# Attention, soft mixture of experts and a gated output layer on one core: a matmul wake-up at the start, two reordered weight loads and a rewritten end of attention

## The chip, the core and the metric

The kernel runs on one core of a Trainium2 chip. TensorE (PE) multiplies, VectorE (DVE), ScalarE (ACT) and GpSimd (POOL) work on tiles in the on-chip memory, and SyncE (SP) does nothing but issue DMA transfers, in program order. Sixteen DMA engines share out every transfer. The metric is the device time of one execution in microseconds. Before the change it is 331.34 us, the median of three runs (331.23, 331.34 and 331.82).

## What is computed

Three stages follow each other on 3072 tokens of 512 columns, all in float32 (the weights `w_in` and `w_out` of the last stage arrive in 64-bit floats and are converted on the chip).

```python
# 1 chunked attention: 4 batches x 8 heads x 768 positions x 64; 24 chunks of 32 queries
for c in range(nc):                       # each chunk sees 8 memory keys and up to 56 keys around it
    scores = scale * np.matmul(q_c, k_full.transpose(0, 1, 3, 2))
    a = softmax(scores)                   # max subtracted, exp, divided by the sum + 1e-9
    out[:, :, c_start:c_end] = np.matmul(a, v_full)
x = attn_out as [3072, 512]
# 2 soft mixture of 8 experts with 4 slots each
logits = x @ phi                          # [3072, 32]
d = softmax over the 3072 tokens;  slot_input = d.T @ x
slot_out[e] = np.maximum(slot_input[e] @ w1[e], 0.0) @ w2[e]
x = softmax over the 32 slots @ slot_out
# 3 output layer
h = x @ w_in;  solu = h * softmax(h);  ln = layer norm of solu * g_ln
return ln @ w_out
```

## The kernel before

Attention runs over 32 groups (`GROUPS`), each of 3 tiles of 128 query rows, for one pair of heads in half a batch. One block of keys and queries (`load_qk`, line 187, 400 KB) is loaded for each group into one of four buffers, and one block of values for two groups (`load_v`, line 201, two transfers of 390 KB) into one of two buffers. The loop over `g` issues, in this order: the scores of group g+1 (`emit_qk`, PE, L281), its softmax on DVE and ACT, the load of the keys four groups ahead, weight loads as the list `LOADS[g]` says (in units of 512 KB), the product with the values of group g-1 (`emit_pv`, PE, L337), for even g the load of the values two to three groups ahead, then transposes (`emit_t` L319, `emit_xt` L348) and copies. `emit_spread` copies the keys into a padded layout three groups ahead (ACT L326, DVE L328, POOL L330). Every four groups form a half batch `hb`, for which the logits (`emit_lg`, L360), their running maximum, and a rescaled sum of slot inputs (`emit_dacc`, L407 and L421) are made.

After the loop the last three groups are finished by hand, the four partial sums are merged (`merge_max`, `merge_sum`, `merge_end`) and `emit_slots` gives the slot inputs. Then the 16 half experts run (`emit_w1` L524, `emit_ht` L531, `emit_w2` L542), with the conversion of `w_out` and the softmax over slots beside them. Then the last stage runs over 24 tiles on PE (L747).

The order of everything is the order of the code (`tc.manual_schedule`). Weights go into slots of 512 KB or 1 MB (`load_e`, lines 255 and 258); a slot is used again when `release` says that its weights were consumed. When attention has used a buffer for the last time, its room is given to weights too: `ex0` is the room of the keys, `ex1` that of the values, `ex2` and `ex3` two of the blocks `x`. A transfer is issued when its target is free and when the transfer eight places ahead of it has landed; SP waits there, and everything behind it on SP's queue waits with it.

```python
LOADS = [0, 0, 0, 2, 0] + [0, 2] * 6 + [0, 1] + [0, 2] * 5 + [99, 99, 0, 0]
...
            if g + 4 < GROUPS:
                load_qk(g + 4)
            load_e(LOADS[g])
            if 1 <= g:
                emit_pv(g - 1)
            if g % 2 == 0 and 0 < g and g // 2 + 1 < GROUPS // 2:
                load_v(g // 2 + 1)
```

Of the kernel before, what the change touches and what calls it, by code (L numbers as in the profile page):

```python
# [43 lines left out]
LOADS = [0, 0, 0, 2, 0] + [0, 2] * 6 + [0, 1] + [0, 2] * 5 + [99, 99, 0, 0]  # L44
# [3 lines left out]
C_ID, C_I4, C_REP, C_NM, C_PHI, C_G = 0, 128, 160, 288, 289, 417  # L48
NCONST = 425
# [16 lines left out]
TORD = [1, 0]  # L66
TKEEP = [2, 1]
# [11 lines left out]
def tile_kernel(ctx: ExitStack, tc: tile.TileContext, kr, vr, w1, w2, w_in, w_out, cst, out):  # L79
# [323 lines left out]
    def emit_dacc(hb, b=7, steps=(0, 1)):  # L403
        n = 32 * GT
        alpha = alphas[hb % 2]
        for t in range(GT if 0 in steps else 0):
# [3 lines left out]
        if 1 not in steps:  # L410
            return
        if hb == 0:
            dve.tensor_copy(out=acc[0:n], in_=bank(b)[0:n])
        else:
            (pool if hb < HB - 1 else dve).tensor_scalar(
                out=ssum[0:n], in0=ssum[0:n], scalar1=alpha[0:n], scalar2=snews[hb % 2][0:n],
                op0=ALU.mult, op1=ALU.add,
            )
            if hb == HB - 1:
                merge_sum()  # L420
            dve.scalar_tensor_tensor(  # L421
                out=acc[0:n], in0=acc[0:n], scalar=alpha[0:n], in1=bank(b)[0:n], op0=ALU.mult, op1=ALU.add
            )
# [398 lines left out]
    with tc.manual_schedule():  # L822
        for i in range(4):
            (pool if i < 3 else dve).memset(at("vz", 2 * VS * i, 2 * VS), 0.0)
            if i < 2:
                dve.memset(kz[i][0:64, KS:2 * KS], 0.0)
                dve.memset(kz[i][64:128, 0:KS], 0.0)
        load_qk(0)
        act.dma_start(out=at("cst", 0, NCONST), in_=cst)
# [5 lines left out]
        load_e(2)  # L835
# [28 lines left out]
        for g in range(GROUPS):  # L864
            if g + 1 < GROUPS:
                emit_qk(g + 1)
# [19 lines left out]
            if g + 1 < GROUPS:  # L886
                emit_exp(g + 1)
# [10 lines left out]
        area("x2", [("ex2", 1024)])  # L898
        more("ex2", 1)
        emit_softmax(GROUPS + 1)  # L900
        emit_dmax(HB - 2)
        emit_xt(GROUPS - 3)
        emit_pv(GROUPS - 1)
        emit_dexp(HB - 2)
        emit_softmax(GROUPS + 2)
        emit_xt(GROUPS - 2, 0)
        if TORD[0]:
            emit_xt(GROUPS - 1, 1)
        emit_turned_pe([dtb, ptb])
        emit_turned_act([Db, l_of(HB - 2)])  # L910
        if not TORD[0]:
            emit_xt(GROUPS - 1, 1)
# [107 lines left out]
def layout(inputs):  # L1020
# [31 lines left out]
    c = np.zeros((P, NCONST), f)  # L1052
# [2 lines left out]
    c[p, C_I4 + p % 32] = 1.0
    for r in range(4):
        c[p, C_REP + 32 * r + p % 32] = 1.0
# [26 lines left out]
```

## Time and profile before

| what | value |
|---|---|
| median of three runs | 331.34 us |
| the profiled execution, its own time | 331.76 us |
| its span in the trace | 330.0 us (1.76 us lie around it) |
| PE busy | 298.8 us, 91% |
| DVE / ACT / POOL busy | 72% / 67% / 51% |
| chain that ended last, by engine | PE 61%, DMA 18%, DVE 9% |
| bytes moved by DMA | 95.85 MB |

All times below are microseconds from the start of the span. Attention lasts until about 118, the experts until 171, the last stage from there to the end. The busy share of PE is an average over stages with different limits, and its matmuls are pipelined, so 91% busy is not 91% of its peak. The stage by stage view is in the stretches and in the chain of waits.

### The profile page before, as it was taken

To read this page: it belongs to the slowest core of one execution; us is meant where nothing else is said; L and a number is where in the kernel's file an instruction comes from. 1 tells how busy PE (TensorE), PEld (TensorE's weight loads), DVE (VectorE), ACT (ScalarE), POOL (GpSimd) and SP (SyncE) were. 2 spreads that over 40 slices of the span, in tenths; PEclk is the share of its full clock that TensorE was granted. 3 is DMA by queue.
4 is the path that set the end of the run, shared out by engine and by line. 5 is a ranking of instruction groups with operands and counts; after the bars stand their busy time and mean duration, and the time that the engine had idled before them with its cause. 6 is when DMAs were issued, how large, how long until landed. Compare 5 with 4: busy or idle time off the path is not lost.

```text
span 330.0 us, 8289 instructions
## 1 busy us (share of the span) xinstructions
PE 298.8 (91%) x3069; PEld 217.0 (66%) x3069; DVE 236.9 (72%) x431; ACT 222.5 (67%) x441; POOL 169.1 (51%) x395
## 2 busy tenths in 40 slices
PE   2787989898898799879899899999999999999996
PEld 2576767677676433333335688888888888888885
DVE  6675888886877339998027986888878788787540
ACT  3566756865775446785326789998888888888721
POOL 5255577666675022233100457777767676666600
PEclk9999999999999999999999999999999999999999
DMA  7999999999999999999930005675656756576521
GB/s 291 422 368 411 412 415 420 413 420 414 416 403 412 392 422 428 422 423 423 422 148 0 1 34 195 240 264 199 234 218 219 251 203 219 219 237 238 194 95 65
DMA packets 32696, 95.85 MB, mean 290 GB/s; under 512 B 3856, under 2 KB 14480, under 8 KB 28944
## 3 DMA queue, kind: packets, MB, share of 16 engines
q1 hardware_dynamic: 32512, 95.11, 74.0%
q8 instruction: 24, 0.39, 0.5%
q10 hardware_dynamic: 144, 0.22, 0.2%
q14 instruction: 16, 0.13, 0.1%
HBM read 78.53 MB, written 16.78 MB: 289 GB/s over the span
## 4 chain that ended last, share of the span: by engine, by line
PE 61%; DMA 18%; DVE 9%; POOL 3%; issue 3%; ACT 2%; SPq 1%; POOLq 0%; ACTq 0%; DVEq 0%
PE bank L747 37%; DMA kq_area<-in_kr_dram 9%; DMA ex_area<-in_w_dram 5%; PE bank L281 5%; PE bank L337 4%; DMA e_area<-in_w_dram 4%; PE h L659 4%; POOL kq_area L330 3%; PE bank L319 2%; SPq L201 1%; PE bank L348 1%; PE bank L360 1%; PE bank L407 1%; PE bank L524 1%; PE bank L757 1%
## 5 line engine op out<-in xcount | busy, mean ns | idle before, releaser
L747 PE MATMUL bank<-wh_area,yh_area 128*128 128x512 f32 x552 | 129.8, 390 | 0.0
L747 PEld LDWEIGHTS bank<-wh_area,yh_area 128*128 128x128 f32 x552 | 103.4, 188 | 21.7
L330 POOL TENSOR_SCALAR kq_area<-kq_area 64x416 f32<-64x416 f32 x88 | 38.3, 440 | 36.2 <-DMA kq_area<-in_kr_dram 21.1
L281 PE MATMUL bank<-kq_area 128*32 128x128 f32 x768 | 29.4, 288 | 14.3 <-POOL kq_area L330 7.3
L322 ACT COPY s_area<-bank 128x384 f32<-128x384 f32 x32 | 15.3, 477 | 32.7 <-PE bank L319 31.4
L730 DVE STREAM_TRANSPOSE yq_area<-yq_area 128x1024 f32<-128x1024 f32 x20 | 24.9, 1245 | 17.2 <-DMA yq_area<-z 17.2
L674 DVE SCALAR_TENSOR_TENSOR eb_area<-h,eb_area 128x1024 f32<-128x1024 f32 x24 | 29.1, 1217 | 9.5 <-ACT eb_area L668 9.2
L281 PEld LDWEIGHTS bank<-kq_area 128*32 128x32 f32 x768 | 20.6, 114 | 20.6 <-POOL kq_area L330 10.7
L299 DVE TENSOR_REDUCE cst_area<-bank 128x6 f32<-128x384 f32 x32 | 17.8, 555 | 19.5 <-PE bank L281 19.0
L337 PE MATMUL bank<-vz_area,s_area 128*32 128x130 f32 x768 | 28.7, 274 | 3.3 <-issue 1.2
L712 POOL TENSOR_SCALAR cst_area<-cst_area 128x1 f32<-128x1 f32 x72 | 26.6, 370 | 7.6
L665 DVE TENSOR_REDUCE cst_area<-h 128x1 f32<-128x1024 f32 x24 | 29.0, 1217 | 0.9 <-PE h L659 0.9
L701 POOL TENSOR_SCALAR cst_area<-cst_area 128x1 f32<-128x1 f32 x24 | 16.9, 705 | 22.4 <-ACT eb_area L668 20.5
L668 ACT ACTIVATE eb_area<-h,cst_area 128x1024 f32<-128x1024 f32 x24 | 26.7, 1112 | 1.9 <-DVE cst_area L665 1.9
L697 ACT ACTIVATE eb_area<-eb_area,cst_area 128x1024 f32<-128x1024 f32 x24 | 27.3, 1139 | 0.1
L694 ACT ACTIVATE eb_area<-eb_area,cst_area 128x1024 f32<-128x1024 f32 x20 | 23.1, 1154 | 4.8 <-DVE eb_area L674 4.3
L741 DVE TENSOR_TENSOR yh_area<-yq_area,yh_area 128x1024 fp32r<-128x1024 f32 x20 | 24.5, 1226 | 2.3 <-ACT yh_area L737 2.3
L337 PEld LDWEIGHTS bank<-vz_area,s_area 128*32 128x32 f32 x768 | 21.6, 108 | 5.8 <-issue 2.2
L737 ACT CAST yh_area<-yq_area 128x1024 fp32r<-128x1024 f32 x20 | 21.0, 1049 | 5.4 <-DVE yq_area L730 5.3
L713 POOL TENSOR_SCALAR cst_area<-cst_area 128x1 f32<-128x1 f32 x72 | 19.9, 276 | 7.1
L765 ACT ACTIVATE eb_area<-bank,cst_area 128x512 f32<-128x512 f32 x23 | 15.8, 687 | 9.7 <-POOL cst_area L703 7.0
L314 ACT ACTIVATE s_area<-s_area 128x384 f32<-128x384 f32 x32 | 16.9, 530 | 2.4 <-DVE s_area L305 2.3
(153 smaller groups left out, 526.9 us busy)
## 6 DMA issues: line engine op xcount, KB each, us to landing
e_area<-in_w_dram SPq DMA_DIRECT2D x15, 1024.0 KB, 10.4
kq_area<-in_kr_dram SPq DMA_DIRECT2D x32, 400.0 KB, 7.3
vz_area<-in_vr_dram SPq DMA_DIRECT2D x32, 390.0 KB, 6.6
ex_area<-in_w_dram SPq DMA_DIRECT2D x10, 1024.0 KB, 14.8
z<-eb_area SPq DMA_DIRECT2D x20, 512.0 KB, 2.8
yq_area<-z SPq DMA_DIRECT2D x80, 128.0 KB, 2.9
out_dram<-eb_area SPq DMA_DIRECT2D x23, 256.0 KB, 2.0
e_area<-in_w_in_dram SPq DMA_DIRECT2D x4, 1024.0 KB, 9.0
```

The costliest lines, as they stand in the source:

```text
L281: pe.matmul(out=bk[32 * j:32 * j + 32, t * 128:(t + 1) * 128], lhsT=kq[i][:, KT + c * CH:KT + (c + 1) * CH], rhs=kwin(g % 2, c), start=Tru ...
L330: pool.tensor_scalar(out=o, in0=i, scalar1=1.0, scalar2=0.0, op0=ALU.mult, op1=ALU.add)
L337: pe.matmul(out=bk[32 * j:32 * j + 32, t * 2 * VW:(t + 1) * 2 * VW], lhsT=atb[g % 2][:, c * CH:(c + 1) * CH], rhs=vz[g // 2 % 2][:, :, g % ...
L665: dve.tensor_reduce(out=sc("nm", i), in_=fin["h"][i % 2], axis=AX.X, op=ALU.max, negate=True)
L668: act.activation(out=eb[i % FIN], in_=fin["h"][i % 2], func=ACTF.Exp, bias=sc("nm", i), accum_out=sc("s", i))
L674: dve.scalar_tensor_tensor(out=ub[i % FIN], in0=fin["h"][i % 2], scalar=-1.0 / FF, in1=eb[i % FIN], op0=ALU.mult, op1=ALU.mult, accum_out= ...
L694: act.activation(out=yb[i % FIN], in_=ub[i % FIN], func=ACTF.Identity, scale=-float(FF), bias=sc("nu", i))
L697: act.activation(out=sq, in_=ub[i % FIN], func=ACTF.Square, scale=-float(FF), bias=sc("nu", i), accum_out=sc("vs", i))
L712: pool.tensor_scalar(out=t, in0=r, scalar1=r, scalar2=xx, op0=ALU.mult, op1=ALU.mult)
L730: dve.transpose(out=yv[i % FIN].rearrange("p (f a t) -> p a f t", f=FC, a=4), in_=yq[i % FIN].rearrange("p (a f t) -> p a f t", f=FC, a=4),)
L741: dve.tensor_tensor(out=yl[i % FIN][:, sl], in0=tps(i, sl) if i < NPE else yv[i % FIN], in1=yh[i % FIN][:, sl].bitcast(FP32), op=ALU.subtract,
L747: pe.matmul(out=fin["o"][i % 2], lhsT=a[i % FIN][:, f * 128:(f + 1) * 128], rhs=w[f], start=start, stop=stop)
```

## The change

1. **Start.** DVE first clears a tile of 128x128, and PE multiplies it by itself 12 times (`WARM`), ahead of the first scores. The result is not used.
2. **Constants.** The constant table loaded by ACT shrinks from 425 to 265 columns; the two index matrices left out of it (`i4`, `i4rep`) are made by two DVE instructions at the end of attention.
3. **First weights.** The first 1 MB of weights is issued behind the keys of group 4 (`LOADS[0] = 2`) and no longer ahead of them.
4. **Last values.** `LOADS[28]` falls from 2 to 0: 1 MB of weights that was issued ahead of the last block of values is issued right behind it.
5. **End of attention.** The exp of the last group is issued ahead of the copy of the group before it, and the last group's own pass leaves the loop. Its products with the values stand directly behind those of group 30, four transposes go into four banks at once, and the sums of half batches 5, 6 and 7 come in a new order. With them the order in which `ex1`, `ex2` and `ex3` become free changes, and so do the sizes in which their weights are loaded. Three matmuls that keep PE busy become one (`TKEEP`).

```diff
-LOADS = [0, 0, 0, 2, 0] + [0, 2] * 6 + [0, 1] + [0, 2] * 5 + [99, 99, 0, 0]
+LOADS = [2, 0, 0, 2, 0] + [0, 2] * 6 + [0, 1] + [0, 2] * 4 + [0, 0, 99, 99, 0, 0]
-NCONST = 425
+NLOAD, NCONST = 265, 425
+WARM = 12
-TORD = [1, 0]
-TKEEP = [2, 1]
+TKEEP = 1
...
+    def dacc_pe(hb, b, db):
+        for t in range(GT):
             pe.matmul(
-                out=bank(b)[32 * t:32 * t + 32, :], lhsT=Db[:, t, :], rhs=xb[hb % 3][:, t, :], start=True, stop=True
+                out=bank(b)[32 * t:32 * t + 32, :], lhsT=db[:, t, :], rhs=xb[hb % 3][:, t, :], start=True, stop=True
             )
...
     with tc.manual_schedule():
+        dve.memset(sb_[0][:, 0:P], 0.0)
+        for _ in range(WARM):
+            pe.matmul(out=bank(7)[:, 0:P], lhsT=sb_[0][:, 0:P], rhs=sb_[0][:, 0:P], start=True, stop=True)
...
-        act.dma_start(out=at("cst", 0, NCONST), in_=cst)
+        act.dma_start(out=at("cst", 0, NLOAD), in_=cst)
...
         load_v(1)
-        load_e(2)
...
+            if g == GROUPS - 2:
+                emit_exp(g + 1)
             emit_at(g)
...
+        emit_softmax(GROUPS)
+        emit_t(GROUPS - 1)
+        emit_at(GROUPS - 1)
+        emit_pv(GROUPS - 2)
         emit_pv(GROUPS - 1)
...
         area("a1", [("ex1", 6 * 1024)])
         more("ex1", 6)
         load_e()
...
+        for i, b in enumerate((3, 2, 0, 1)):
+            emit_xt(GROUPS - 4 + i, b, copy=False)
+            move("ad"[i % 2], xtb[:, i, :], bank(b)[:, 0:GTOK])
...
+        dacc_pe(last_hb - 2, 4, Db)
...
+        area("x2", [("ex2", 1024)])
+        more("ex2", 1)
+        load_e()
...
+        dacc_pe(last_hb - 1, 7, other)
         area("x0", [("ex3", 1024)])
         more("ex3", 1)
         load_e()
```

SP's queue at the start: `kq_area` takes keys, `vz_area` values, `e_area` weights. Before:

```order
L187 DMA kq_area<-in_kr_dram 128x800 x3
L201 DMA vz_area<-in_vr_dram 64x1560 x2
L187 DMA kq_area<-in_kr_dram 128x800
L201 DMA vz_area<-in_vr_dram 64x1560 x2
L258 DMA e_area<-in_w_in_dram 128x1024
```

The same place after the change:

```order
L187 DMA kq_area<-in_kr_dram 128x800
L201 DMA vz_area<-in_vr_dram 64x1560 x2
L187 DMA kq_area<-in_kr_dram 128x800
L258 DMA e_area<-in_w_in_dram 128x1024
L187 DMA kq_area<-in_kr_dram 128x800 x2
```

The fifth block of keys stands ahead of the first weights, where it stood behind them.

SP's queue at the last blocks of keys and values and the weights behind them (`128x2048` is 1 MB, `128x1024` of `in_w_dram` 512 KB). Before:

```order
L187 DMA kq_area<-in_kr_dram 128x800
L255 DMA e_area<-in_w_dram 128x2048
L201 DMA vz_area<-in_vr_dram 64x1560 x2
L255 DMA e_area<-in_w_dram 128x2048 x3
L255 DMA ex_area<-in_w_dram 128x2048 x2
L255 DMA ex_area<-in_w_dram 128x1024 x2
L255 DMA ex_area<-in_w_dram 128x2048 x3
L255 DMA ex_area<-in_w_dram 128x1024
```

The same place after the change:

```order
L187 DMA kq_area<-in_kr_dram 128x800
L201 DMA vz_area<-in_vr_dram 64x1560 x2
L255 DMA e_area<-in_w_dram 128x2048 x4
L255 DMA ex_area<-in_w_dram 128x2048 x2
L255 DMA ex_area<-in_w_dram 128x1024 x2
L255 DMA ex_area<-in_w_dram 128x2048 x2
L255 DMA ex_area<-in_w_dram 128x1024 x3
```

Between the last keys and the last values nothing stands any more, and of the loads into `ex_area` five are half loads where three were. The same eight or nine loads come a second time in the experts, in the same sizes.

PE's queue at the end of attention (`bank_84` to `bank_91` are banks 0 to 7). Before:

```order
L337 MATMUL bank_88<-vz_area,s_area 32x130 x12
L407 MATMUL bank_91<-x_area,s_area 32x512 x3
L360 MATMUL bank_90<-s_area,cst_area 32x128 x12
L319 MATMUL bank_86<-cst_area,s_area 128x128 x3
L348 MATMUL bank_87<-cst_area,x_area 128x128 x6
L337 MATMUL bank_89<-vz_area,s_area 32x130 x12
L348 MATMUL bank_84<-cst_area,x_area 128x128 x3
L348 MATMUL bank_85<-cst_area,x_area 128x128 x3
L394 MATMUL bank_90<-cst_area,s_area 128x96 x2
L360 MATMUL bank_87<-s_area,cst_area 32x128 x12
```

The same place after the change:

```order
L319 MATMUL bank_86<-cst_area,s_area 128x128 x3
L337 MATMUL bank_88<-vz_area,s_area 32x130 x12
L337 MATMUL bank_89<-vz_area,s_area 32x130 x12
L360 MATMUL bank_90<-s_area,cst_area 32x128 x12
L348 MATMUL bank_87<-cst_area,x_area 128x128 x3
L348 MATMUL bank_86<-cst_area,x_area 128x128 x3
L348 MATMUL bank_84<-cst_area,x_area 128x128 x3
L348 MATMUL bank_85<-cst_area,x_area 128x128 x3
L394 MATMUL bank_90<-cst_area,s_area 128x96 x2
L360 MATMUL bank_87<-s_area,cst_area 32x128 x12
```

The two last products with the values stand next to each other, ahead of the sums and the logits; the sum (L407) of half batch 5 has left this place for a later one.

## Rows read from the trace of the kernel before

**Rows 1.** Page, part 2: GB/s of the DMA in 40 slices of 8.25 us.

```profile
GB/s 291 422 368 411 412 415 420 413 420 414 416 403 412 392 422 428 422 423 423 422 148 0 1 34 195 240 264 199 234 218 219 251 203 219 219 237 238 194 95 65
```

**Rows 2.** Chain that ended last: start, us, engine and line, end of the experts.

```profile
156.66 12.19 DMA e_area<-in_w_dram
...
168.89 1.05 PE bank L542 x4
...
187.84 0.23 PE bank L747
```

**Rows 3.** Stretches: busy us (instructions) of PE PEld DVE ACT POOL, clock, DMA share, GB/s.

```profile
17.00:22.00 5.00, 4.05 (x96) 3.24 (x92) 3.56 (x10) 3.81 (x9) 3.13 (x8) 1.00 0.98 340
24.00:96.00 72.00, 63.99 (x1406) 50.05 (x1397) 56.52 (x147) 48.19 (x136) 47.70 (x84) 1.00 1.02 415
113.50:115.50 2.00, 1.67 (x8) 0.68 (x10) 1.06 (x4) 0.53 (x2) 0.00 (x0) 1.00 0.92 293
116.00:166.00 50.00, 44.31 (x347) 16.91 (x346) 34.99 (x80) 29.86 (x70) 12.46 (x13) 1.00 1.01 423
163.50:166.50 3.00, 2.42 (x18) 0.79 (x20) 0.23 (x1) 0.43 (x2) 0.00 (x0) 1.00 1.02 419
```

**Rows 4.** The same view in half microseconds: first bytes, last values, last weights.

```profile
1.50:2.00 0.50, 0.00 (x0) 0.00 (x0) 0.47 (x1) 0.50 (x1) 0.50 (x1) 1.00 0.58 102
...
3.00:3.50 0.50, 0.00 (x0) 0.00 (x0) 0.29 (x1) 0.00 (x0) 0.50 (x2) 1.00 1.09 424
...
98.50:99.00 0.50, 0.50 (x28) 0.44 (x16) 0.47 (x2) 0.29 (x1) 0.41 (x1) 1.00 0.72 267
...
167.00:167.50 0.50, 0.50 (x4) 0.00 (x0) 0.00 (x0) 0.00 (x0) 0.00 (x0) 1.00 0.68 279
...
168.50:169.00 0.50, 0.45 (x4) 0.11 (x4) 0.00 (x0) 0.00 (x0) 0.00 (x0) 1.00 0.35 107
```

**Rows 5.** Chain that ended last, first 24 us: start, us, engine and line.

```profile
5.87 1.54 PE bank L281 x24
...
9.21 0.89 PE bank L319 x3
...
21.50 0.79 PE bank L281 x24
```

**Rows 6.** Timeline: start, us, engine, line, shapes [idle before <-releaser].

```profile
0.72 1.34 SPq L187 DMA_DIRECT2D kq_area<-in_kr_dram  x3
...
13.88 1.88 SPq L201 DMA_DIRECT2D vz_area<-in_vr_dram  x2
...
14.85 0.72 ACT L326 COPY kq_area<-kq_area 64x416 f32<-64x416 f32 x2 [1.55 <-DMA kq_area<-in_kr_dram]
```

**Rows 7.** Timeline of SP's queue at the last keys, weights and values.

```profile
90.93 0.53 SPq L187 DMA_DIRECT2D kq_area<-in_kr_dram  x1
91.50 0.43 SPq L255 DMA_DIRECT2D e_area<-in_w_dram  x1
96.98 1.12 SPq L201 DMA_DIRECT2D vz_area<-in_vr_dram  x2
```

**Rows 8.** Issue to landing: keys issued at 90.93, weights at 91.50, weights at 120.25.

```profile
DMA to landing us min/median/max: 7.5/7.5/7.5
DMA to landing us min/median/max: 9.4/9.4/9.4
DMA to landing us min/median/max: 8.9/8.9/8.9
```

**Rows 9.** Timeline of PE: products with values of groups 27, 30, 31; keeping matmuls.

```profile
96.31 0.64 PE L337 MATMUL bank<-vz_area,s_area 128*32 128x130 f32 x12 [0.37 <-issue]
...
103.37 0.88 PE L337 MATMUL bank<-vz_area,s_area 128*32 128x130 f32 x24 [0.29 <-ACT s_area L322]
...
108.09 0.87 PE L337 MATMUL bank<-vz_area,s_area 128*32 128x130 f32 x24
...
113.23 1.54 PE L554 MATMUL bank<-s_area,cst_area 128*128 128x384 f32 x4
```

More of the change, by code (lines that the diff above doesn't have):

```diff
@@ L401, in l_of, with dacc_sum, dacc_acc, emit_dacc @@
         return L[:, hb * GT:hb * GT + GT, :]
[L403 to L406, printed above, removed]
+    def dacc_pe(hb, b, db):
+        for t in range(GT):
             pe.matmul(
-                out=bank(b)[32 * t:32 * t + 32, :], lhsT=Db[:, t, :], rhs=xb[hb % 3][:, t, :], start=True, stop=True
+                out=bank(b)[32 * t:32 * t + 32, :], lhsT=db[:, t, :], rhs=xb[hb % 3][:, t, :], start=True, stop=True
             )
-        if 1 not in steps:
-            return
+    def dacc_sum(hb, eng):
+        eng.tensor_scalar(
+            out=ssum[0:NR], in0=ssum[0:NR], scalar1=alphas[hb % 2][0:NR], scalar2=snews[hb % 2][0:NR],
+            op0=ALU.mult, op1=ALU.add,
+        )
+    def dacc_acc(hb, b):
+        dve.scalar_tensor_tensor(
+            out=acc[0:NR], in0=acc[0:NR], scalar=alphas[hb % 2][0:NR], in1=bank(b)[0:NR], op0=ALU.mult, op1=ALU.add
+        )
+    def emit_dacc(hb):
+        dacc_pe(hb, 7, Db)
         if hb == 0:
-            dve.tensor_copy(out=acc[0:n], in_=bank(b)[0:n])
+            dve.tensor_copy(out=acc[0:NR], in_=bank(7)[0:NR])
         else:
[L415 to L423, printed above, removed]
+            dacc_sum(hb, pool)
+            dacc_acc(hb, 7)
     def merge_max(b=6):
@@ L863, in tile_kernel @@
         )
-        for g in range(GROUPS):
-            if g + 1 < GROUPS:
-                emit_qk(g + 1)
+        for g in range(GROUPS - 1):
+            emit_qk(g + 1)
             if g == GROUPS - 2:
@@ L897, in tile_kernel @@
                 early[j][i]()
[L898 to L902, printed above, removed]
-        emit_pv(GROUPS - 1)
[L904 to L912, printed above, removed]
+        last_hb = HB - 1
+        other = at("s", 0, GT * NSLOT).rearrange("p (t s) -> p t s", s=NSLOT)
+        emit_softmax(GROUPS)
+        emit_t(GROUPS - 1)
+        emit_at(GROUPS - 1)
+        emit_pv(GROUPS - 2)
+        emit_pv(GROUPS - 1)
         area("a1", [("ex1", 6 * 1024)])
@@ L915, in tile_kernel @@
         load_e()
-        emit_lg(HB - 1, 3)
-        emit_dacc(HB - 2, steps=(0,))
+        emit_softmax(GROUPS + 1)
+        emit_lg(last_hb - 1, copy=False)
+        emit_softmax(GROUPS + 2)
+        emit_dmax(last_hb - 1)
+        emit_lgcopy(last_hb - 1)
+        for i, b in enumerate((3, 2, 0, 1)):
+            emit_xt(GROUPS - 4 + i, b, copy=False)
+            move("ad"[i % 2], xtb[:, i, :], bank(b)[:, 0:GTOK])
+            if i == 0:
+                emit_dexp(last_hb - 1, scale=False)
+        emit_scale(last_hb - 1)
+        emit_turned_pe([dtb, ptb])
+        emit_turned_act([other, l_of(last_hb - 1)])
+        emit_lg(last_hb, 3)
+        dve.tensor_reduce(out=i4, in_=ident.rearrange("p (r s) -> p s r", r=4), axis=AX.X, op=ALU.add)
+        dve.tensor_copy(
+            out=i4rep.rearrange("p (r s) -> p r s", r=4),
+            in_=i4.rearrange("p (o s) -> p o s", o=1).to_broadcast([P, 4, 32]),
+        )
+        dacc_pe(last_hb - 2, 4, Db)
+        dacc_sum(last_hb - 2, pool)
+        emit_dmax(last_hb, 3)
+        merge_max()
+        dacc_acc(last_hb - 2, 4)
+        area("x2", [("ex2", 1024)])
+        more("ex2", 1)
+        load_e()
+        emit_dexp(last_hb, 3, scale=False)
+        emit_turned_pe([dtb], 2)
+        emit_turned_act([Db], 2)
+        emit_scale(last_hb)
+        merge_scale()
+        dacc_pe(last_hb - 1, 7, other)
         area("x0", [("ex3", 1024)])
@@ L1051, in layout @@
     a["w_out"] = np.ascontiguousarray(inputs["moe2_w_out"].reshape(FC, P, DM)).view(np.int64)
[L1052 removed]
+    c = np.zeros((P, NLOAD), f)
     p = np.arange(P)
     c[p, C_ID + p] = 1.0
[L1055 to L1057 removed]
     c[(p // 32) % 2 == 1, C_NM] = -1.0
```

21 lines of the change are left out of this document (9 added, 12 removed).

## Prediction, made before the changed kernel was run

> **What bounds the kernel now.** I read the bytes per slice first, then the chain of waits from its end, then the stretches where the DMA rate falls. The slices [rows 1] show about 415 GB/s from the second slice to the twentieth, some 165 us, and next to nothing for 30 us after that: attention and experts are one stream of loads. The chain says that this stream sets the end [rows 2]: a weight load lands at 168.85 (156.66 + 12.19), PE starts the last products with w2 at 168.89, and the last stage on L747 begins at 187.84. From 168.85 on the change leaves everything as it is, so those 161 us are fixed, and the question is how the landing at 168.85 moves. Until then the 16 DMA engines are full: 415 GB/s at a share of 1.02 from 24 to 96, and 423 GB/s at 1.01 from 116 to 166 [rows 3]. What PE, DVE or ACT do sooner inside attention is worth nothing unless it fills a hole in the stream. The holes are few: 340 GB/s from 17 to 22, 293 GB/s from 113.5 to 115.5 [rows 3], and a share of 0.72 from 98.5 to 99 [rows 4].
>
> **Constants, 0.2 us less.** 160 columns of 4 bytes on 128 partitions are 82 KB; at 415 GB/s [rows 3] that is 0.2 us out of the stream. The two DVE instructions that build the matrices instead lie in the end of attention, covered as below.
>
> **Start: between nothing and 0.9 us less; I take 0.4.** The clock column reads 1.00 all along, but the same 24 score matmuls take 1.54 us at 5.87 and 0.79 at 21.5 [rows 5]: the first ones run at the lower of the two levels, 1.2 GHz, after an idle PE. The change puts 12 matmuls of 128x128 ahead of them. No row shows one. From below, three transposes of that size at the lower level take 0.89 us [rows 5], so 12 take 3.6. From above, two matmuls of 384 columns take 1.54 us at the higher level [rows 9]; a third of the columns at half the clock makes 0.51 each, 6.2 us for 12. PE starts them near 1.2, behind DVE's small clear, and is free between 4.8 and 7.4; the scores waited until 5.87. So the first scores end between 0.75 us sooner (1.54 less 0.79) and 1.5 us later (7.4 against 5.87, at the lower level still). The clear also stands ahead of DVE's other clears, some 0.2 us; that is inside these bounds.
>
> What this reaches is SP: the third block of values is issued at 13.88 [rows 6], when a product with the values has ended, and behind it on SP stand all later loads. The hole from 17 to 22 follows; it is worth 5 us x (1 - 340/415) = 0.9 us. Sooner scores move that issue up and fill part of it. The fifth block's keys, now 1 MB (2.5 us) nearer the front, remove ACT's 1.55 us wait at 14.85 [rows 6]; but the sixth block has the same bytes ahead of it as before and is the next late thing, so this is worth nothing by itself. The moved load has 3.4 MB ahead of it by the code (constants, four blocks of keys, two of values), 8 us of transfers, so SP does not run dry while it waits. I take half of the hole, 0.4 us, nearer to the rows at full rate on both sides than to none.
>
> **The last values: between nothing and 2.5 us more; I take 0.8.** This is the term that speaks against the change. Before, SP issues the last keys at 90.93, 1 MB of weights at 91.50, and then waits with the last values until 96.98 [rows 7], when PE ends a product that reads their buffer (96.31 + 0.64) [rows 9]. The keys land at 98.4 (90.93 + 7.5), the weights at 100.9 (91.50 + 9.4) [rows 8]. So that megabyte is what the engines chew while SP waits. Even with it some ran dry: share 0.72 from 98.5 to 99 [rows 4]. After the change it stands behind the values, and everything behind the waiting SP stands with it. The pipeline up to there is paced by the same bytes, so neither the wait nor the issue moves against the stream; I expect an issue at about 96.8 and no bytes of it before about 99: at the start of the kernel the first issue at 0.72 [rows 6] moves 102 GB/s from 1.5 to 2.0 and full rate only from 3.0 [rows 4], 2.3 us later.
>
> How much of that reaches the end? If all engines lost it, the whole transfer: 1.05 MB at 419 GB/s [rows 3] is 2.5 us. But the engines do not finish together: the rate falls from 279 GB/s at 167 to 107 at 168.5 [rows 4], so a landing is set by the latest of them, 2 us behind the first. The latest one ends the last keys at 98.4 and lacks work for only 0.6 us before 99. If it is also the latest at the end, the loss is 0.6 or nothing. Against that, after the hole all engines start level and must spread again. I take 0.8, near the latest engine's own gap, and keep both ends.
>
> Here a page would put the sum lower. The Trainium skill, page "DMA: Bandwidth & Descriptors", section "Latency and other measured facts", gives about 0.6 us to the first byte of a hardware-generated DMA; by it the values would flow from 97.4, no engine that ends its keys at 98.4 would see a gap, and the sum below would be 0.8 us less. The trace does not bear it out: its first bytes come at least 0.8 us after the first issue, and full rate after 2.3.
>
> **Half loads: between 0.6 us less and 2.2 more; I take 0.1 more.** The new order in which `ex1`, `ex2` and `ex3` come free makes five half loads of three, in each of two rounds: 4 more, 2.1 MB. Where halves alone are moved the trace shows 419 GB/s from 163.5 to 166.5 and 293 from 113.5 to 115.5 [rows 3]. Against 4.96 us at the 423 GB/s around them, 2.1 MB cost 5.01 by the first, 0.1 more at most, and 7.2 by the second, 2.2 more. If the slow stretch does not come again it gives back 2 us x (1 - 293/423) = 0.6. The longer stretch is the one at the stream's usual rate, so I take that.
>
> **End of attention: nothing.** The product of group 31 moves from 108.09 [rows 9] to right behind that of group 30 at 103.37, which now waits for ACT alone and hardly for its values. Two or three microseconds of it may reach the first expert. But what is late next is the stream, which is full there. In the other direction there is cover: the first load that waits for a consumed weight is issued at 120.25 and lands 8.9 us later [rows 8]; less its own 1.3 us (512 KB at 419 GB/s) and 2.3 to start, some 5 us of other loads stood ahead of it. The rewritten end, with its two extra DVE instructions, may be 5 us later before the stream notices. One keeping matmul instead of three: 1.5 us of PE on no path.
>
> **Sum.** -0.2 - 0.4 + 0.8 + 0.1 = +0.3. The profiled execution took 331.76 us, 1.76 around a span of 330.0; it should become 332.1 with a span of 330.3. It lies 0.4 above the median, so I put the median at 331.34 + 0.3 = **331.6**. About 0.2%, 0.66 us, is what a measurement here can tell from no change: 330.7 to 332.0.
>
> **Rivals.**
> *The hole costs every engine (slower).* Place: SP's wait for the last values' buffer. If the start-up of 2.3 us counts in full and all engines end the keys near 97, they idle 2 us and start level; then -0.2 - 0.4 + 2.0 + 0.1 = +1.5, 332.8. It decides as soon as the landing at the end moves by more than the latest engine's 0.6 us. For it: the dip at 98.5 and the 2.5 us of work that is missing there. Against it: the spread of the landings. Chance 0.25.
> *The wake-up is too long (slower).* The 12 matmuls end at 7.4, the third block of values is issued 1.5 us late, and the hole from 17 to 22 doubles: +0.9 in place of -0.4, in all +1.6, 332.9. Against it: ten microseconds of loads stand ahead by then. Chance 0.07.
> *The stream loses its holes (faster).* The start fills the whole 0.9, the slow stretch at 113.5 does not come again (0.6), and the latest engine sees no gap at 98: -0.2 - 0.9 - 0.6 + 0.1 = -1.6, 329.7; half of it, 330.5, is as likely. For it: two of the three holes lie where orders change. Chance 0.24.
> *The change does not reach the end at all*, every part beside a stream of the same bytes: -0.1, 331.2. That lies inside the forecast's own range, 330.9 to 332.0.
>
> **How the numbers follow.** Forecast with its quiet neighbour 0.44, slower rivals together 0.32, faster 0.24. The chances of faster, same and slower are these. The range leaves out about one in ten on either side: 330.2, below the half-way faster case, and 333.0, above both slower ones.
>
> **What would show it.** Right: last weights landing near 169.1, L747 starting near 188.1, a share well under 1 between 97 and 99 in place of full engines, and the rest of the stream at 420. The start is right if the first 24 score matmuls take 0.8 us and 17 to 22 moves more than 340 GB/s. Wrong: a landing at 170 or later with the hole at 97 as its only cause; or one before 168.3, which would mean that holes were filled that I counted on. If the landing stays and the end moves, the fixed 161 us were not fixed.

## The result and the profile after

The changed kernel takes 335.74 us, the median of four runs, and the kernel before 331.28 us in runs beside it: a ratio of 1.0122 (95% interval 1.0084 to 1.0161), 4.1 us slower by the ratio and 4.5 by the medians. 331.6 was predicted, with a range up to 333.0. The profiled execution took 335.61 us with a span of 333.5, against 331.76 and 330.0.

The chain of waits of the changed kernel, at the end of the experts (start, us, engine and line; L545 and L750 are L542 and L747 of before):

```profile
161.02 10.98 DMA e_area<-in_w_dram
...
172.04 1.05 PE bank L545 x4
...
190.98 0.23 PE bank L750
```

It is the chain of [rows 2], later by 3.15 us: PE takes up the last w2 at 172.04 instead of 168.89, and the last stage starts at 190.98 instead of 187.84. What follows is 0.36 us longer (142.52 against 142.16 us to the end of the span), and 0.35 us more lie around the span. So the loss is in the stream, ahead of the landing. The page's GB/s in 40 slices of 8.3 us, to be held against [rows 1], say where:

```profile
GB/s 290 420 359 364 419 413 419 415 416 406 412 338 351 423 416 424 426 423 420 423 222 0 1 34 157 252 177 265 224 252 190 248 229 213 224 231 241 202 84 63
```

Slices 3 and 4 fell from 368 and 411 to 359 and 364, slices 12 and 13 from 403 and 412 to 338 and 351. The same in stretches (columns as in rows 3: clock, DMA share and GB/s stand last), before:

```profile
16.00:22.00 6.00, 5.05 (x128) 4.24 (x131) 3.74 (x10) 4.17 (x10) 3.13 (x8) 1.00 1.00 359
22.00:28.00 6.00, 5.29 (x132) 4.27 (x128) 4.65 (x14) 3.62 (x10) 1.88 (x5) 1.00 1.03 408
96.00:105.00 9.00, 7.87 (x161) 5.94 (x163) 7.76 (x21) 5.26 (x16) 6.66 (x10) 1.00 0.99 398
105.00:118.00 13.00, 10.34 (x118) 6.02 (x112) 6.00 (x20) 4.71 (x17) 0.34 (x1) 1.00 1.00 401
```

and after:

```profile
16.00:22.00 6.00, 3.48 (x56) 2.71 (x55) 1.61 (x5) 3.13 (x7) 3.26 (x9) 0.72 1.03 413
22.00:28.00 6.00, 5.88 (x138) 4.70 (x135) 5.35 (x14) 3.99 (x10) 1.93 (x4) 1.00 0.86 277
96.00:105.00 9.00, 7.44 (x159) 5.88 (x154) 7.56 (x21) 5.92 (x19) 7.50 (x12) 1.00 0.82 282
105.00:118.00 13.00, 11.26 (x146) 6.84 (x144) 7.80 (x25) 4.03 (x16) 0.34 (x1) 1.00 1.00 417
```

Each stretch loses (length) x (1 - GB/s / 415). From 16 to 28 that was 0.81 + 0.10 = 0.9 us before and is 0.03 + 2.00 = 2.0 now: **1.1 more**. From 96 to 105 it was 0.4 and is 2.9: **2.5 more**. From 105 to 118 it was 0.4 and is nothing: **0.5 less**. With 0.2 us of constants less this makes +2.9 of the 3.15; the other 0.25 is a slightly slower stream from 40 to 90 (414 GB/s, where it was 416).

**The first hole.** SP's queue and PE at the start of the changed kernel (start, us, engine, line; in brackets the idle time before, and what ended it; the profile has two records for each of these matmuls, so a group's 12 score matmuls are x24):

```profile
12.95 1.25 SPq L201 DMA_DIRECT2D vz_area<-in_vr_dram  x2
14.31 0.52 SPq L187 DMA_DIRECT2D kq_area<-in_kr_dram  x1
...
21.83 1.12 SPq L201 DMA_DIRECT2D vz_area<-in_vr_dram  x2
```

```profile
1.03 4.60 PE L828 MATMUL bank<-s_area 128*128 128x128 f32 x24 [1.03 <-DVE s_area L826]
6.01 1.52 PE L281 MATMUL bank<-kq_area 128*32 128x128 f32 x48 [0.38 <-ACT kq_area L326]
...
15.23 0.43 PE L337 MATMUL bank<-vz_area,s_area 128*32 128x130 f32 x7 [0.43 <-issue]
...
18.98 1.51 PE L281 MATMUL bank<-kq_area 128*32 128x128 f32 x24 [2.52 <-POOL kq_area L330]
20.26 1.50 PE L337 MATMUL bank<-vz_area,s_area 128*32 128x130 f32 x24
```

The 12 matmuls of the wake-up end at 5.63 (1.03 + 4.60), and the first two groups of scores then take 1.52 us together. The third block of values is issued at 12.95, 0.9 us sooner than in [rows 6], as forecast, and the hole at 17 is gone. But the fourth block is issued at 21.83; in the kernel before it was 20.76, and PE had two shorter waits:

```profile
20.76 1.12 SPq L201 DMA_DIRECT2D vz_area<-in_vr_dram  x2
```

```profile
15.89 0.86 PE L281 MATMUL bank<-kq_area 128*32 128x128 f32 x24 [1.60 <-POOL kq_area L330]
...
19.17 0.86 PE L281 MATMUL bank<-kq_area 128*32 128x128 f32 x24 [0.95 <-POOL kq_area L330]
19.85 0.85 PE L337 MATMUL bank<-vz_area,s_area 128*32 128x130 f32 x24
```

Now PE waited 2.52 us for the keys of the sixth group, and then ran that group at half speed, 1.51 us for scores that take 0.86 in the rows above (0.79 in the chain of [rows 5]). The keys themselves did not move: they land at 17.2 before the change (8.7 + 8.5) and at 17.1 after it (8.0 + 9.1), and the scores behind them start at 19.17 and 18.98. The later issue is the slow group: its scores and the product behind them, which frees the buffer, take 1.51 and 1.50 us where they took 0.86 and 0.85, about 1.3 us more, less the 0.2 by which the scores start sooner. The granted clock agrees, 0.55 from 18 to 20; the same view in smaller windows, with the second hole:

```profile
18.00:20.00 2.00, 1.02 (x20) 0.96 (x24) 0.00 (x0) 1.86 (x4) 1.63 (x4) 0.55 1.04 423
...
97.00:98.00 1.00, 1.00 (x23) 0.80 (x12) 1.00 (x3) 0.44 (x2) 0.85 (x3) 1.00 0.56 217
98.00:99.00 1.00, 1.00 (x29) 0.83 (x31) 0.96 (x4) 0.85 (x3) 1.00 (x1) 1.00 0.47 108
99.00:101.00 2.00, 1.65 (x38) 1.21 (x29) 1.97 (x6) 1.01 (x4) 1.42 (x4) 1.00 0.81 278
101.00:103.00 2.00, 1.48 (x48) 1.23 (x48) 1.76 (x6) 1.33 (x5) 1.78 (x4) 1.00 0.96 291
103.00:105.00 2.00, 1.40 (x15) 1.11 (x11) 1.82 (x7) 1.29 (x5) 1.54 (x2) 1.00 0.90 340
```

**The second hole.** The last keys are issued at 91.94 and the last values at 97.61:

```profile
91.94 0.53 SPq L187 DMA_DIRECT2D kq_area<-in_kr_dram  x1
97.61 1.28 SPq L201 DMA_DIRECT2D vz_area<-in_vr_dram  x2
```

The engines run partly dry from 97 to 99, which costs 1.2 us, and then the stream does not come back at its rate: 99 to 105 at 278 to 340 GB/s costs another 1.6.

### The profile page after: what moved, and what is told of

It reads as the page before. It is cut to its first block, busy times and chain, and to the rows that moved or that the text cites. A ratio compares the mean times of both kernels' runs of the same rounds, so it can differ in the third digit from the quotient of the medians.

```text
span 333.5 us, 8335 instructions
## 1 busy us (share of the span) xinstructions
PE 303.4 (91%) x3089; PEld 220.0 (66%) x3089; DVE 239.5 (72%) x436; ACT 221.9 (67%) x439; POOL 169.1 (51%) x395
## 4 chain that ended last, share of the span: by engine, by line
PE 54%; DMA 35%; DVE 4%; POOL 3%; ACT 2%; issue 1%; SPq 1%; POOLq 0%; ACTq 0%
PE bank L750 36%; DMA e_area<-in_w_dram 12%; DMA ex_area<-in_w_dram 10%; DMA kq_area<-in_kr_dram 9%; DMA vz_area<-in_vr_dram 4%; PE h L662 4%; PE bank L281 3%; PE bank L337 3%; POOL kq_area L330 2%; PE bank L319 1%; PE bank L760 1%; PE t L760 1%; PE t L719 1%; PE bank L360 1%; PE bank L405 1%
## 5 line engine op out<-in xcount | busy, mean ns | idle before, releaser
L750 PE MATMUL bank<-wh_area,yh_area 128*128 128x512 f32 x552 | 129.8, 390 | 0.0
L750 PEld LDWEIGHTS bank<-wh_area,yh_area 128*128 128x128 f32 x552 | 103.4, 188 | 21.8
L715 POOL TENSOR_SCALAR cst_area<-cst_area 128x1 f32<-128x1 f32 x72 | 26.6, 370 | 7.6
L281 PEld LDWEIGHTS bank<-kq_area 128*32 128x32 f32 x768 | 19.8, 111 | 16.1 <-POOL kq_area L330 12.2
L716 POOL TENSOR_SCALAR cst_area<-cst_area 128x1 f32<-128x1 f32 x72 | 25.1, 348 | 7.1
L704 POOL TENSOR_SCALAR cst_area<-cst_area 128x1 f32<-128x1 f32 x24 | 13.5, 564 | 26.3 <-ACT eb_area L671 24.4
```

The lines of the kernel that those rows point to most:

```text
L281: pe.matmul(out=bk[32 * j:32 * j + 32, t * 128:(t + 1) * 128], lhsT=kq[i][:, KT + c * CH:KT + (c + 1) * CH], rhs=kwin(g % 2, c), start=Tru ...
L715: pool.tensor_scalar(out=t, in0=r, scalar1=r, scalar2=xx, op0=ALU.mult, op1=ALU.mult)
L716: pool.tensor_scalar(out=r, in0=t, scalar1=1.5, scalar2=r, op0=ALU.add, op1=ALU.mult)
L750: pe.matmul(out=fin["o"][i % 2], lhsT=a[i % FIN][:, f * 128:(f + 1) * 128], rhs=w[f], start=start, stop=stop)
```

## The experiments

Every kernel ran beside the kernel before on the same chip; the times below are (ratio - 1) x 332 us over it, with the 95% interval. The expectations call the load issued at 20.76 before "the third load of values"; counted as in the prediction it is the fourth block.

**The loads put back.** From the changed kernel:

```diff
 a1: edit 4 undone
-LOADS = [2, 0, 0, 2, 0] + [0, 2] * 6 + [0, 1] + [0, 2] * 4 + [0, 0, 99, 99, 0, 0]
+LOADS = [2, 0, 0, 2, 0] + [0, 2] * 6 + [0, 1] + [0, 2] * 5 + [99, 99, 0, 0]
 a2: edit 3 undone
-LOADS = [2, 0, 0, 2, 0] + ...
+LOADS = [0, 0, 0, 2, 0] + ...
         load_v(1)
+        load_e(2)
 a3: both undone
 a4: edit 1 undone, no clear and no 12 matmuls
```

> The changed kernel with edit 4 alone undone: 1 MB of weights stands ahead of the last values again. Theory (two separate holes, one per moved load): the hole at 96 to 105 closes (398 GB/s there, as before the change, where the changed kernel has 282), the clock still falls near 18 and the hole at 22 to 28 stays (about 277 GB/s); 9 x (398 - 282) = 1.04 MB, 2.5 us at 415 GB/s, so 335.7 - 2.5 = 333.2. Rival (the prediction's size for this edit, 0.8 us, with the rest of the loss elsewhere): 334.9. Rival (the stream is late from the first hole on, and the second would come in any order): 335.5 or more.

> The changed kernel with edit 3 alone undone: the first 1 MB of weights stands ahead of the fifth block of keys again; the wake-up stays. Theory (edit 3 joins two short waits of PE into one of 2.5 us, after which the clock is low for one group of scores and values, and the third load of values is issued 1 us late): clock 1.00 from 18 to 22, that load issued at 20.7 or sooner, about 408 GB/s from 22 to 28, and 335.7 - 1.2 = 334.5. Rival (the wake-up ahead of the scores is what brings the clock down at 18): the clock falls at 18 all the same, and the time stays at 335.4 or more.

> The changed kernel with edits 3 and 4 undone: wake-up, shorter constants and the new end of attention remain. Theory (the loss is these two edits', the rest gives 0.2 for constants, 0.5 for the slow stretch at 113.5 that does not come again, and up to 0.4 at the start): 330.3 to 330.9, faster than the kernel before (331.3). Rival (the new end of attention or its additional half loads cost): 331.5 or more.

> The changed kernel with edit 1 alone undone: no clear and no 12 matmuls ahead of the first scores. Theory (the clock falls because of the wait for the sixth block of keys, whatever came first): the clock falls near 18 again, hole at 22 to 28 as in the changed kernel, 335.5 to 336.2. Rival (the wake-up brings the fall): clock 1.00 at 18, no hole at 22, about 334.4.

| kernel | over before, us | 16 to 22, GB/s | 22 to 28 | 96 to 105 |
|---|---|---|---|---|
| a1, edit 4 undone | +1.1 (0.4 to 1.8) | 414 | 267 | 407 |
| a2, edit 3 undone | +4.4 (3.2 to 5.6) | 415 | 233 | 282 |
| a3, both undone | +1.0 (0.1 to 1.9) | 420 | 227 | 396 |
| a4, no wake-up | +3.6 (2.6 to 4.6) | 294 | 406 | 335 |

The second hole is edit 4's and goes with it; a1 against the changed kernel makes 2.5 to 3.0 us. The theory on the first hole fell: with edit 3 undone the hole is there, and larger, and the clock falls all the same. Among these four it is absent at 22 only without the wake-up, where another stands at 16 instead. So edit 1 puts it there, not edit 3, and a3, the wake-up with the rest harmless, is slower than the kernel before, against the theory's 0.4 to 1.0 us less.

**Single edits on the kernel before, and the end alone.** d1 is the changed kernel with edits 1, 3 and 4 undone; b3 and e4 are the kernel before with one edit:

```diff
 b3: edit 4 alone
-LOADS = [0, 0, 0, 2, 0] + [0, 2] * 6 + [0, 1] + [0, 2] * 5 + [99, 99, 0, 0]
+LOADS = [0, 0, 0, 2, 0] + [0, 2] * 6 + [0, 1] + [0, 2] * 4 + [0, 0, 99, 99, 0, 0]
 e4: edit 1 alone
     with tc.manual_schedule():
+        dve.memset(sb_[0][:, 0:P], 0.0)
+        for _ in range(12):
+            pe.matmul(out=bank(7)[:, 0:P], lhsT=sb_[0][:, 0:P], rhs=sb_[0][:, 0:P], ...)
```

> The kernel before with edit 4 alone: 1 MB of weights stands behind the last values instead of ahead of them. Theory (edit 4 is the larger loss by itself; side by side it was 2.9 and 3.5 us with the other edits around it): a share of 0.5 or less in two microseconds near 97 to 99, a restart near 300 GB/s behind it, 96 to 105 at 280 to 340 GB/s where the kernel before has 398; 2.0 to 3.3 us more than the kernel before. Rival (the hole needs the wake-up's or the new end's timing): 0 to 0.8 more.

> The kernel before with edit 1 alone: DVE's clear and 12 matmuls ahead of the first scores. Theory (the third load of values waits for the sixth block of keys, which no wake-up brings sooner; the bytes ahead of that load are used up sooner, PE waits in one piece of 3 to 4 us and the clock falls behind it): 16 to 22 above 405 GB/s, the third load of values issued at 21.5 to 22.6 where it was 20.76, 22 to 28 at 220 to 340 GB/s; 0.7 to 1.9 us more than the kernel before. Rival (the wake-up alone gains what was predicted for the start): 0.4 less.

> The changed kernel with edits 1, 3 and 4 undone: only the shorter constants and the new end of attention with its half loads stand against the kernel before. Theory: 0.2 less for the constants and between 0 and 0.5 less for the slow stretch near 114; the start reads as in the kernel before: 0.2 to 0.7 us less than it. Rival (the 1.0 us that the kernel with wake-up, constants and end lost against the kernel before came from the end): 0.8 to 1.0 more.

Measured: b3 +1.8 (0.9 to 2.7), e4 +0.6 (-0.4 to 1.6), d1 +0.1 (-0.7 to 0.9). Edit 4 is the larger loss by itself too, with 96 to 105 at 289 GB/s; its price is a little under what was expected. The end of attention with its half loads and the shorter constants show no cost or gain within the interval of d1, so what a3 lost is more likely the wake-up's than the end's. In the trace the wake-up alone makes the hole that the theory says. SP, PE and two stretches of e4:

```profile
13.07 1.92 SPq L201 DMA_DIRECT2D vz_area<-in_vr_dram  x2
...
23.76 1.12 SPq L201 DMA_DIRECT2D vz_area<-in_vr_dram  x2
```

```profile
17.30 1.51 PE L281 MATMUL bank<-kq_area 128*32 128x128 f32 x24 [3.81 <-POOL kq_area L330]
```

```profile
16.00:22.00 6.00, 4.70 (x66) 3.77 (x70) 1.84 (x5) 2.48 (x7) 3.21 (x8) 0.51 1.03 414
22.00:28.00 6.00, 6.00 (x152) 5.14 (x144) 4.81 (x13) 4.83 (x12) 2.40 (x6) 0.92 0.64 205
```

PE has its first scores at full speed, reaches the fifth group 0.8 us sooner than in the kernel before (13.49 against 14.29), and waits 3.81 us in one piece for its keys; behind that wait the granted clock is 0.51 from 16 to 22, and the fourth block of values goes out at 23.76. Not all of that wait comes from PE being early: the fifth block's keys land at 16.1, and at 14.8 in the kernel before. In a2 and a3, with the wake-up and the same order of loads, it is 16.0 and 16.2; in b3 and d1, without the wake-up, 14.7 and 14.6. Why they land later is open. In time e4's loss is 0.6 us, just below the 0.7 to 1.9 of the theory, and the interval does not exclude none.

**Filling the wait.** If the low clock makes the hole, PE must be kept busy in the wait:

```diff
         for g in range(GROUPS - 1):
+            if g == 4:
+                for _ in range(12):
+                    pe.matmul(out=bank(7)[:, 0:P], lhsT=ident, rhs=ident, start=True, stop=True)
             emit_qk(g + 1)
```

b1 and f2 are the changed kernel with these lines, on two chips; c1 has edit 4 undone besides; f1 is the changed kernel itself beside f2.

> The changed kernel with 12 more matmuls of 128x128 (constant operands, result unused) on PE ahead of the scores of the sixth group, in the 2.5 us in which it waits there; nothing else differs. Theory after the first four runs (the wake-up makes PE finish sooner what the keys allow, the wait for the next keys comes in one piece, the clock falls behind it, one group runs at half clock and the third load of values is issued 1.1 us late): the clock stays 1.00 from 16 to 24, that load is issued near 20.8, and most of the hole at 22 to 28 closes (277 GB/s to 380 or more, 1.5 us of the 2.0): 1.5 us less than the changed kernel, which in runs side by side lies 4.1 above the kernel before, so +2.6. Rival (the low clock only accompanies a stream that runs dry anyhow, because the bytes ahead of that load are used up by 22): the hole stays and so does the time, +3.8 to +4.4.

> The changed kernel with edit 4 undone and the same 12 matmuls in the wait ahead of the sixth group's scores. Theory: no hole at 16 to 28 beyond some 0.4 us (the kernel before has 0.9 there) and none at 97; with the shorter constants (0.2) and, where the slow stretch near 114 does not come, 0.5 more: 0.7 to 1.2 us less than the kernel before. Rival (the new end of attention and its half loads cost something): the same as the kernel before or more.

> The changed kernel itself, beside the three others on one chip. Both theories: some 4 us more than the kernel before. If the low clock makes the hole at 22 to 28, executions whose mean clock is 0.998 or more are 1 us shorter than those below it; if it only accompanies the hole, they are alike.

> The changed kernel with the 12 matmuls in the wait ahead of the sixth group's scores (the kernel of b1_keep), side by side with the changed kernel. Theory (the low clock is half of the hole): 0.9 to 1.4 us less than the changed kernel. Rival (it only accompanies it; the issue of the third load of values after the bytes ahead are used up makes the hole): 0.3 less or nothing.

Measured: b1 +2.7 (1.9 to 3.5), c1 +1.3 (0.3 to 2.3), f1 +3.6 (2.5 to 4.6), f2 +3.0 (1.9 to 4.0). b1 is where the theory put it in time (+2.6), but its hole closed only to 341 GB/s and not to 380. In all six executions of f2 the clock stayed up, but it gained 0.6 us on f1 and not 0.9 to 1.4, with intervals that overlap, and c1 missed its 0.7 to 1.2 us less altogether. PE in c1:

```profile
17.04 0.43 PE L338 MATMUL bank<-vz_area,s_area 128*32 128x130 f32 x7 [1.60 <-issue]
...
18.11 2.84 PE L873 MATMUL bank<-cst_area 128*128 128x128 f32 x24
20.88 0.86 PE L282 MATMUL bank<-kq_area 128*32 128x128 f32 x24
```

PE stopped for 1.60 us in the middle of a product with values, on nothing that this view shows (the last section comes back to it), so the 2.84 us of filling began late and pushed the scores to 20.88. The fourth block went out at 22.47 and 22 to 28 moved 249 GB/s, at a granted clock of 1.00: it is the late issue that makes the hole, by whatever cause. The filling is a fixed piece of work for a wait that is not fixed. f1 shows the same stop in the changed kernel itself, in an execution where the clock stayed up:

```profile
16.96 0.43 PE L337 MATMUL bank<-vz_area,s_area 128*32 128x130 f32 x7 [1.95 <-issue]
...
18.98 0.86 PE L281 MATMUL bank<-kq_area 128*32 128x128 f32 x24 [0.79 <-POOL kq_area L330]
```

```profile
16.00:22.00 6.00, 4.25 (x95) 3.44 (x98) 2.38 (x8) 3.97 (x10) 3.35 (x8) 1.00 1.02 415
22.00:28.00 6.00, 6.00 (x157) 5.04 (x152) 5.67 (x16) 4.66 (x11) 2.22 (x6) 1.00 0.96 344
```

Here the scores run at full speed from 18.98, the fourth block is issued at 20.57, and the hole at 22 is half as large: 1.0 us where the other execution lost 2.0, and the kernel before 0.9 from 16 to 28. f1's executions took 334.31 and 334.49 us with a mean clock of 0.998 or more and 335.55 to 336.08 in the four below that, 1.4 us apart. In the first comparison, though, the one execution at 1.0 took 335.65, no less than the others. So about half of the first hole stands without the low clock, as much as the kernel before had there; that the other half is the clock's is read from the two traces, and in time it is likely and not settled. A long wait is not always followed by the lower level either: b3's PE waited 2.05 us and its scores took 1.51, b2's stopped for 2.21 us and its scores took 0.86.

**The next late thing moved.** What holds PE up next is the sixth block of keys. In e1 the first 1 MB goes behind it, with edit 4 undone; e2 is e1 without the wake-up; f3 is e1 with edit 4 as changed; f4 puts 2 MB ahead of the last values. b2 is the changed kernel with 512 KB there:

```diff
 e1: LOADS = [0, 2, 0, 2, 0] + [0, 2] * 6 + [0, 1] + [0, 2] * 5 + [99, 99, 0, 0]
 f3: LOADS = [0, 2, 0, 2, 0] + [0, 2] * 6 + [0, 1] + [0, 2] * 4 + [0, 0, 99, 99, 0, 0]
 f4: LOADS = [0, 2, 0, 2, 0] + [0, 2] * 6 + [0, 1] + [0, 2] * 4 + [0, 4, 99, 99, 0, 0]
 b2: LOADS = [2, 0, 0, 2, 0] + [0, 2] * 6 + [0, 1] + [0, 2] * 4 + [0, 1, 99, 99, 0, 0]
```

> The changed kernel with edit 4 undone and the first 1 MB of weights moved one block of keys further back, behind the sixth block. Theory (the third load of values waits for the sixth block's keys, and these for the megabyte ahead of them): those keys land 2.5 us sooner, PE does not wait 2 us ahead of the sixth group's scores, the clock stays 1.00, the third load of values is issued at 18 to 19.5, and nothing is left of the hole from 16 to 28 (at least 400 GB/s in both halves): 0.8 to 1.4 us less than the kernel before. Rival (something else is next late there, a copy of the keys or the instructions of PE, and that load stays near 20.7 or later): the same as the kernel before or up to 1 more.

> The same kernel without the wake-up. Theory (the wake-up is worth something only once the keys no longer hold PE up): PE reaches the second load of values' release 1 to 2 us later, at 14 to 15.5, a hole of 0.9 to 1.7 us stays at 16 to 22, and none at 22 to 28: between 0.2 less and 0.8 more than the kernel before, some 1 us more than with the wake-up. Rival (the wake-up is worth nothing here either): the same time as with it.

> The changed kernel with half of edit 4 undone: 512 KB of weights stands ahead of the last values, where the kernel before has 1 MB and the changed kernel nothing. Theory (each byte that is missing while SP waits is idle time of all engines, and the restart behind it, at some 300 GB/s for 5 us, is part of the price): half a megabyte fills 1.3 of the 2 us at 97 to 99, and with a shorter hole the slow restart shrinks too; 1.3 to 2.2 us less than the changed kernel, +1.9 to +2.8 over the kernel before. Rival (the slow restart is a fixed price of any hole): only 1.2 us less, and 99 to 105 stays near 300 GB/s. Rival (the prediction's: only the latest engine counts, and it lacked 0.6 us): the hole costs nothing more, +1.2.

> The changed kernel with the first 1 MB behind the sixth block of keys, and edit 4 as it is in the changed kernel: the hole at 97 with nothing lost ahead of it. Theory (edit 4's price is 2 us of idle engines and a restart near 300 GB/s): 2.0 to 2.9 us more than the kernel with the same start and edit 4 undone, which lay 1.0 below the kernel before; so +1.0 to +1.9. Rival (half of edit 4's loss was a late pipeline from the first hole): 1.0 to 1.6 more than it, +0.0 to +0.6.

> The same start with 2 MB of weights ahead of the last values, where the kernel before has 1 MB and the changed kernel none. Theory (half a megabyte closed the hole nearly whole, 1 MB leaves 0.35 us at 96 to 105): 96 to 105 at 405 GB/s or more, and a time within 0.4 us of the kernel with 1 MB, 0.6 to 1.3 below the kernel before. Rival (the last values land 2.5 us later and the products of the last groups wait for them): 0.5 to 2 us more than with 1 MB.

| kernel | over before, us | ahead of the last values | 16 to 22, GB/s | 22 to 28 | 96 to 105 |
|---|---|---|---|---|---|
| e1 | -1.0 (-2.0 to -0.1) | 1 MB | 414 | 403 | 399 |
| e2, no wake-up | -0.4 (-1.3 to 0.5) | 1 MB | 297 | 408 | 416 |
| f3 | +1.8 (0.9 to 2.8) | nothing | 411 | 422 | 355 (206 from 95 to 96) |
| f4 | -0.7 (-1.5 to 0.1) | 2 MB | 417 | 421 | 417 |
| b2 | +1.6 (1.0 to 2.3) | 512 KB | 412 | 299 | 410 |

e1 is faster than both kernels, by as much as was expected, with an interval that just excludes none; f4's gain is of the same size, but its interval does not. SP, PE and the stretches of f4:

```profile
18.04 1.12 SPq L201 DMA_DIRECT2D vz_area<-in_vr_dram  x2
```

```profile
16.45 0.86 PE L281 MATMUL bank<-kq_area 128*32 128x128 f32 x24
```

```profile
16.00:22.00 6.00, 5.15 (x113) 4.00 (x111) 4.25 (x12) 4.45 (x11) 1.50 (x4) 1.00 1.03 417
22.00:28.00 6.00, 4.51 (x125) 3.98 (x126) 3.87 (x12) 4.17 (x10) 2.44 (x6) 1.00 1.03 421
96.00:105.00 9.00, 6.33 (x136) 4.93 (x137) 6.98 (x18) 5.23 (x15) 6.07 (x8) 1.00 1.01 417
105.00:118.00 13.00, 10.70 (x133) 6.37 (x124) 7.80 (x25) 3.42 (x15) 0.39 (x2) 1.00 1.02 424
```

The sixth group's scores start at 16.45 with no wait in front, the fourth block of values goes out at 18.04 instead of 21.83, and no stretch is under 417 GB/s. That shows the mechanism: the keys that wait behind a megabyte of weights set the issue of the values, and that sets the hole. With the keys out of the way the wake-up seems worth about 0.7 us, not the 1 expected (e1 against e2, whose intervals overlap). In e1's own profiled execution PE stopped in the same place for 1.95 us, the fourth block went out at 20.08, and the stream still held 403.

The amounts ahead of the last values do not price by the byte. b2's 512 KB, 1.3 us of transfers, closed the whole hole in its trace, 410 GB/s where nothing ahead gives 282 to 355 in eight traces; what its trace still shows is the first hole, 299 GB/s at 22 to 28. Its expectation named 1.3 to 2.2 us of gain over the changed kernel; against f1's +3.6, on another chip, it is 2.0. Over the kernel before it named +1.9 to +2.8, and the 1.6 lies below that. f3 against e1 and f4, with the same start, prices edit 4 at 2.5 to 2.8 us.

## Why the prediction was wrong

Every term is held against the change in lost time of the profiled pair.

**Bound: right.** One stream until the last w2, then a nearly fixed rest (0.36 us longer in the span, 0.35 around it; these two are not explained).

**Start: -0.4 predicted, +1.1 measured.** The wake-up worked: the first scores run at full speed and the third block of values moved from 13.88 to 12.95, which filled the hole at 17 to 22. The step that failed is "Sooner scores move that issue up and fill part of it": it follows one load and stops there. A hole that is filled by sooner bytes comes back at the next load that did not move, and that is the fourth block, which waits for the sixth group's keys: they land at 17.1 as before, and in f1, at full clock, 1.0 us is missing at 22 to 28 where 0.9 was missing from 16 to 28. The prediction named those keys as the next late thing, but only to value edit 3 at nothing; it did not carry them into the wake-up. The second half was not thought of at all: PE's earlier work collects its waits in one piece (2.52 us, where it was 1.60 and 0.95), behind that piece the granted clock is the lower level, and the group on which the load depends runs at half speed, which puts its issue 1.1 us later than before the change. e4 shows both with the wake-up alone, f4 shows the hole gone once the keys come sooner.

**Edit 3: nothing predicted.** With the wake-up it seems to gain up to 0.9 us (f1 against a2), with edit 4 undone nothing (a1 against a3); it is not the cause that the first theory made of it.

**Last values: +0.8 predicted, +2.5 measured** in this pair, 1.8 to 3.5 in the others. The place, the wait and the dry stretch at 97 to 99 were right, and 2.5 was the upper bound. The step that failed is the latest engine's "lacks work for only 0.6 us". The share of 0.56 and 0.47 in the two microseconds from 97 to 99 says that half of the engines' time was idle, while the latest engine had hardly a gap: the last packet of the keys starts at 98.81 and the first of the values at 98.86. The stream's end moved by the whole hole all the same and not by one engine's gap. The term also held nothing for the restart, 1.6 of the 2.8 us. The rival "the hole costs every engine", at 2.0, was near; its 0.25 was too little. The first-byte figure that the prediction weighed, 0.6 us in the Trainium skill, page "DMA: Bandwidth & Descriptors", section "Latency and other measured facts", would have the values flow at 98.2. Their first packet starts at 98.86, 1.25 us after the start of the issue at 97.61, and it is 1.25 or 1.26 us in the seven other traces with nothing ahead of the last values; counted from there, these traces do not bear the figure out.

**Half loads: +0.1 predicted, -0.5 measured.** The slow stretch near 114 did not come in this execution (422 GB/s from 113.5 to 115.5), which was close to the term's lower bound, 0.6 less. In a1, with the same half loads, the stretch from 105 to 118 moved 406 GB/s, so this is timing rather than a gain of the edit.

**End of attention: nothing predicted, nothing found.** d1, which holds it and the constants, is at +0.1 (-0.7 to 0.9). **Constants: -0.2,** too small to be seen alone.

**The sign "wrong" came true:** a landing after 170, though with two holes, where only the one at 97 was foreseen. The sign that the start is right came true as well (0.76 us for 24 records of scores, 411 GB/s from 17 to 22), and the start was wrong: the sign looked at the one load that the prediction had followed.

## What to carry to other kernels

When a load sequence is bound by a stream, ask of every saved microsecond which load it moves and what the next load after that one waits for; if that is a transfer with the same bytes ahead of it, the hole only moves back. Put what unblocks the issuing queue (here keys) ahead of what nobody waits for yet (weights), and keep some of such weights ahead of any load that has to wait for a buffer; here half a megabyte was enough, in one trace. It lasts 1.3 us at 415 GB/s, about the 1.25 us from the start of an issue to its first packet. Price a gap together with its restart, which here cost more than the gap itself.

## What the runs showed of the hardware beyond that

**A restart is slow.** After two partly dry microseconds the stream ran at 278 to 340 GB/s for six, with a share of 0.81 to 0.96, although SP issued three megabytes from 98.94 to 100.4 and a fourth at 102.9. The packets of the trace show two parts of it. From 98.86 to 101.37 only packets of the values move (6240 bytes), 0.69 MB in all; the first packet of the weights issued at 98.94 (8192 bytes) starts at 101.37. Behind that, until 105, three packets of 8192 bytes take 1.8 us and nine 0.50 to 0.91, where most take 0.31; such an engine counts as busy and moves less. After the first hole it was alike: 22 to 28 at 277 with SP issuing again from 21.83. Why the weights start so late and why single packets take so long is open; no run was made for it.

**PE stopped in the middle of a product.** In every kernel with both the wake-up and the new place of the first megabyte, PE stops in the middle of the same product, after 17 of its 24 records, in ten traces: 0.43 us in the changed kernel, 1.95 in f1, 1.60 in c1, 2.21 in b2. The DMA view of f1 from 14.5 to 17 has an instruction transfer there:

```profile
q8 instruction: 1, 0.02, 2.6%
```

The Trainium skill, page "Runtime: NRT & Kernel Launch", section "Instruction fetch mechanics", tells of refills in blocks of 16 KiB and calls their cost mostly hidden. The size agrees with the 0.02 MB; the cost was not hidden here. The ten traces tie the stop to this transfer: it starts anywhere from 12.83 (changed kernel) to 15.18 (b2), and the product goes on 2.2 to 2.5 us behind that start in all ten; where the transfer starts late, the stop is long. Why it starts at such different times, and what fills the 2.2 us of which the transfer itself takes 1.0, is open, and no run moved it on purpose.

**The clock's rise varies between executions of the same code.** Kernels without the wake-up run the same instructions on PE until 9 us, yet the three transposes on L319 at 9.19 took 0.55 us in b3 and 0.89 in the kernel before [rows 5], and in a4 those at 12.76 still took 0.90:

```profile
9.19 0.55 PE L319 MATMUL bank<-cst_area,s_area 128*128 128x128 f32 x3 [0.54 <-ACT s_area L314]
```

```profile
12.76 0.90 PE L319 MATMUL bank<-cst_area,s_area 128*128 128x128 f32 x3
```

The clock column reads 1.00 there all the same; the durations tell the level. In a4 this moved the third block of values to 15.43 and made the hole at 16 (294 GB/s); e2 is alike, 15.37 and 297. The kernel before spread over 330.0 to 334.9 us on the three chips of the experiments, and b3's early rise was followed by the same fall of the clock that the wake-up brings.
